# Attention with chunk selection and an ELU MLP: every batch in three query blocks, two head pairs to a PSUM bank

## The chip, the core and the metric

The kernel runs on one core of one Trainium2 chip. The metric is the device time of one execution in microseconds (us). The engines are named as the profile names them: PE (TensorE, matrix multiplies), PEld (its weight loads), DVE (VectorE), ACT (ScalarE), POOL (GpSimd) and SP (SyncE, which here only issues transfers). PSUM is the memory that PE writes and that DVE and ACT read; a bank of it holds 512 float32 numbers on each of 128 partitions.

## The reference

Four batches, eight heads, 768 positions, 64 numbers per head. Keys are cut into chunks of 32; for each query the six chunks with the highest upper bound are kept, and attention runs over those alone, causally. The result, as 3072 rows of 512, goes through an MLP with an ELU between its two products.

```python
chunk, top_k = 32, 6
k_min, k_max = k_chunks.min(axis=3), k_chunks.max(axis=3)
ub = sum(maximum(q * k_min, q * k_max), axis=-1)      # one bound for each query and chunk
top_chunks = argsort(where(causal, ub, -1e9))[..., -top_k:]
scores = where(selected & causal, (q @ k.T) / 8, -1e9)
attn = softmax(scores) @ v
x = attn.transpose(0, 2, 1, 3).reshape(3072, 512)
h = x @ w_in                                          # 512 x 2048
g = where(h > 0, h, exp(minimum(h, 0)) - 1)
out = g @ w_out                                       # 2048 x 512
```

## The kernel before

The work goes block by block. A block is one batch and a range of its queries; `CUTS` (L36) gives batch 0 three blocks of 256 queries and the other batches two of 384, nine blocks in all. The eight heads are handled as four head pairs (`NPAIR`), numbered j: two heads of 64 numbers fill the 128 partitions.

For each block these steps run, each of them a function that records operations:

- **Loads** (`load`, L449 on): 128 queries of all eight heads at a time, 256 KB each, of K, Q and V. For the first three blocks most of them are issued by POOL, and each such issue keeps POOL for about 0.9 us; all later ones are issued by SP. The weights of the MLP are loaded by POOL too, behind the loads of block 1.
- **Preparing K** (`prep_k`, one head pair at a time): PE turns the tiles into one PSUM bank (L501), DVE takes the maximum and the minimum of each chunk of 32 keys (both at L521), and ACT copies the bank out, narrowed to bf16: for blocks 0 and 1 straight into `lhs` (L528, two copies, one for each head), for the others into `kb` (L533), from which SP sends two transfers to `lhs` (L536).
- **Preparing Q** (`prep_q`, one head pair at a time): PE turns the tiles (L501), ACT copies them to `QTf` (L548), two casts bring them to bf16 in `rhs` (for blocks 0 and 1 by ACT, L553, else by POOL, L561), and DVE makes `Qrl`, the positive part (L564).
- **Selecting** (`select`): PE multiplies Q with the chunk bounds (L586, float32), and DVE transposes the result (L597), finds the six best chunks of each query (L604), compares (L608) and transposes the mask into the rows of `rhs` that stand under the queries. Blocks 0 to 2 do that last step with DVE alone (L614); later blocks go through `msk` (L620) and SP transfers (L624).
- **Attending** (`attend`, one head pair at a time): scores (L649; in blocks 0 and 1 the causal triangle is added by a further product, L652), the exponential on ACT (L668, L672), the causal triangle on DVE (L681, L688), the product with V (L703) into one shared bank `o_bank`, the division on DVE (L712, L714) and a transpose into `xt`: for block 0 and the last block by PE (L722) with a copy by DVE (L725), for all others by one transposing transfer on SP's queue (L727).
- **MLP** (`mlp`): 16 slices of 128 of the hidden layer. PE multiplies (L744, four products a slice, as wide as the block has queries); then exp on ACT (L748), an addition on POOL (L750) and the larger or smaller of the two on DVE (L752). Where a block is 256 wide, two slices share a bank and these three run 512 wide. Then each 128 queries are multiplied with `w_out` (L765, sixteen products 512 wide), copied out by ACT (L769) and stored by SP (L772).

The order of all this is not the order of the program text. Each operation is recorded with an engine, an estimated duration, its dependencies and a priority (`plan.op`). `Plan.run` then lets a model of the engines, the transfer queues and the buffers (`CAPS` gives the number of each kind) choose, operation by operation, what each engine does next; the instructions are written in that order, and each engine works through its own list strictly in order. The table `SHIFTS` moves priorities, one number for each kind of operation, engine and block. Operations on one PSUM buffer are put in a chain: a reader waits for the reader before it. Where the model leaves PE idle in the first 70 us, small products on a tile named `junk` are put in (L886).

The front of block i+2 (loads, preparation, selection) is recorded while block i attends, and the MLP of block i stands one block behind.

Of the kernel before, what the change touches and what calls it, by code (L numbers as in the profile page):

```python
# [15 lines left out]
B = 4  # L16
# [19 lines left out]
CUTS = [(0, 256, 512, 768)] + [(0, 384, 768)] * (B - 1)  # L36
BLOCKS = [(b, x, lo, hi) for b in range(B) for x, (lo, hi) in enumerate(zip(CUTS[b], CUTS[b][1:]))]
NBLK = len(BLOCKS)
QMAX = 384
# [25 lines left out]
CAPS = dict(psO=1, psM=7, kld=2, qld=2, vld=1, QTf=6, Qrl=6, kb=3, kmx=2, ubT=2, thr=2,  # L65
            msk=2, pt=9, rcp=2, on=3, xt=12, gT=6, e=4, osb=2)
# [3 lines left out]
EARLY = 30e3  # L70
# [4 lines left out]
    ('cast', 'POOL'): (0.36301, -2.6351, -5.23122, -9.94413, 7.65777, -0.20339, -5.07548, -2.54865, 4.34574),  # L75
    ('gate', 'POOL'): (3.67964, 0.0, 0.0, 0.0, 0.0, 0.0, 0.0, 0.0, 0.0),
    ('init', 'DVE'): (-0.26172, 0.0, 0.0, 6.20378, 8.3173, 3.17992, 8.6172, 2.93233, 6.71757),
    ('init', 'POOL'): (-1.0933, 3.47219, 0.0, 0.0, 0.0, 4.52292, 0.0, 0.0, 0.0),
    ('init', 'SP'): (0.0, 0.0, -0.65038, 0.0, 0.0, 0.0, 0.0, 0.0, 0.0),
    ('kld', 'ACT'): (4.45058, 0.0, 0.0, 0.0, 0.0, 0.0, 0.0, 0.0, 0.0),  # L80
    ('kld', 'SP'): (-2.34682, 0.0, 0.0, 4.79323, 4.52046, -2.14229, -6.13817, -3.59852, -2.65828),
    ('kld', 'POOL'): (0.0, -6.75562, 5.09695, 0.0, 0.0, 0.0, 0.0, 0.0, 0.0),
    ('mlp_in', 'ACT'): (-2.40904, -3.14044, -3.25982, -5.32754, -5.81099, 0.10442, -5.22457, -3.10776, -7.20826),
    ('mlp_in', 'DVE'): (-1.35758, -0.66733, 4.05424, -3.97602, -2.37476, -2.51264, 6.24384, 1.43361, 1.4263),
    ('mlp_in', 'PE'): (2.58869, 0.18485, -0.03717, -4.42605, -1.68403, 0.1887, -0.63691, 0.32029, -2.51407),
    ('mlp_in', 'POOL'): (4.31076, -0.7994, -0.08548, -2.64871, -12.83076, -3.46529, -9.26201, -2.48698, -1.52442),
    ('mlp_out', 'ACT'): (1.82419, -3.05015, -0.78962, -5.55384, -0.16865, -5.05754, 1.41655, -1.16262, -6.87802),
    ('mlp_out', 'PE'): (0.24075, 0.17459, 0.14942, -0.16027, 6.11871, 0.1171, 7.22562, 0.28947, -0.95423),
    ('mlp_out', 'SP'): (-1.76499, -1.716, 5.02829, 3.79669, 6.31947, 8.72257, -1.57087, 0.64556, -8.37831),
    ('prep_k', 'ACT'): (-0.13258, -2.29432, -5.21413, -5.81582, 0.31577, -1.55852, -0.71998, -0.96509, 5.07829),  # L90
    ('prep_k', 'DVE'): (5.88483, 11.93445, -1.39572, -5.21965, -4.45086, -1.35195, -0.53949, -1.64957, -3.66217),
    ('prep_k', 'PE'): (1.96837, 5.99494, 0.08442, 0.09507, 5.41155, -0.21367, -1.89727, 0.49894, 0.29539),
    ('prep_k', 'SP'): (0.0, 0.0, -1.97489, 0.08999, 1.60003, 1.51775, -0.18511, 2.62204, 0.88012),
    ('prep_q', 'ACT'): (-1.1238, -0.17378, -4.62395, -0.38281, -5.63326, -4.36887, 0.60622, 5.30204, 1.20927),
    ('prep_q', 'DVE'): (-1.10909, -11.65783, -10.30533, -1.22248, -15.41771, -10.30347, -8.05233, -0.05077, -3.91546),
    ('prep_q', 'PE'): (-1.9696, -3.23903, -0.01361, -2.1371, -6.53782, -2.99976, -0.67109, 0.13649, 0.01158),
    ('prep_q', 'POOL'): (0.0, 0.0, 11.59933, 3.13777, 1.34215, 2.81799, 3.74405, 9.94498, 5.00197),
    ('qld', 'ACT'): (1.21441, 0.0, 0.0, 0.0, 0.0, 0.0, 0.0, 0.0, 0.0),
    ('qld', 'SP'): (3.66104, 0.0, 0.0, -0.9899, 2.54606, 3.7401, 9.93352, 1.39708, -3.02005),
    ('qld', 'POOL'): (0.0, 3.13091, -1.26946, 0.0, 0.0, 0.0, 0.0, 0.0, 0.0),  # L100
    ('score', 'ACT'): (-7.56297, 0.20574, 8.91891, -5.01381, -2.59914, -0.36508, 1.44839, 2.2134, 3.41788),
    ('score', 'PE'): (0.62726, 0.20683, -0.02773, 0.15303, -0.32678, -2.74631, 0.19235, -0.05167, 0.25745),
    ('score', 'DVE'): (0.0, 0.0, -0.41053, 3.75163, -5.17063, -0.00102, -1.63319, 2.60448, -5.59281),
    ('select', 'DVE'): (-0.39483, -11.74184, -0.31948, -2.00715, -2.53616, -1.49369, 0.2018, 5.38174, -1.32975),
    ('select', 'PE'): (-3.8939, -8.46886, -9.81244, -9.94423, -3.54113, -5.76916, -5.21074, -7.35482, -7.76008),
    ('select', 'SP'): (0.0, 0.0, 0.0, 0.30026, -0.34655, -1.66126, 2.46548, 9.84369, -1.93244),
    ('vld', 'POOL'): (-1.40633, -3.20526, -8.56927, 0.0, 0.0, 0.0, 0.0, 0.0, 0.0),
    ('vld', 'SP'): (0.0, 0.0, 0.0, 0.46689, -0.0871, 2.09994, 4.64846, 3.54379, -2.03203),
    ('w_in', 'POOL'): (-2.40508, 0.0, 0.0, 0.0, 0.0, 0.0, 0.0, 0.0, 0.0),
    ('w_out', 'POOL'): (-6.04092, 0.0, 0.0, 0.0, 0.0, 0.0, 0.0, 0.0, 0.0),  # L110
    ('weigh', 'DVE'): (6.56984, 1.9914, -4.71512, -3.33812, 2.4539, -0.73675, 4.35514, -1.94984, 0.73236),
    ('weigh', 'PE'): (8.24559, -1.30337, -3.1578, -2.868, -0.84271, -0.35438, -0.13752, 4.33018, -0.6965),
    ('weigh', 'SP'): (0.0, -2.66794, -8.47684, -0.40249, -1.54504, -3.77342, -5.02577, -2.38304, 0.0),
# [15 lines left out]
def dve_ns(n):  # L129
    return 68 + 1.03 * n  # L130
# [24 lines left out]
class Plan:  # L155
# [38 lines left out]
    def run(self):  # L194
# [42 lines left out]
        while True:  # L237
# [43 lines left out]
            if done is not None:  # L281
                done.end = clock + (1100 if clock < EARLY else DMA_END)
                lanes[done.eng][done.lane] = done.end
                dirty.update(("SP", "ACT", "POOL"))
                leave(done, done.end)
                enter(done, done.end, True)
                continue
# [28 lines left out]
            else:  # L316
                o.end = t + o.occ + o.lat + (50 if t < EARLY else MARGIN)
# [7 lines left out]
def kernel(  # L325
# [44 lines left out]
    lhs = [fix([P, 2, S], BF16, f"lhs{s}") for s in range(NSET)]  # L370
# [125 lines left out]
    def turn_in(ps, ld, nt):  # L496
        xb, r, hs = ld

        def go():
            for n in range(nt):  # L500
                nc.tensor.transpose(ps.get()[:, P * n:P * (n + 1)],  # L501
                                    xb.get()[:, n, hs, :].rearrange("p h d -> p (h d)"), ident_f)

        op("PE", 15 + 107 * nt, 200, go, reads=[*r, r_ident_f], writes=[ps], hold=[xb])

# [3 lines left out]
    def prep_k(j, i):  # L509
        plan.tag = ("prep_k", i)  # L510
        b, x, lo, hi = BLOCKS[i]
        s, bp, w = (NPAIR * b + j) % NSET, b % 2, hi - lo
        nch = w // CHUNK
        cs = slice(lo // CHUNK, hi // CHUNK)
        k_ld = ldk.pop((j, i))
        psk = buf("psM" if i in PSM_PREP else PS_T, [P, QMAX], F32)
        turn_in(psk, k_ld, w // P)
        kmx = tops[i] = tops[i] if j else buf("kmx", [P, NPAIR, QMAX // CHUNK], F32)

        def reduce(out, o):  # L520
            nc.vector.tensor_reduce(out=out, in_=psk.get()[:, 0:w].rearrange("p (c w) -> p c w", w=CHUNK),  # L521
                                    axis=AX.X, op=o)
# [260 lines left out]
    def front(i):  # L783
        at = span(i - 1, *SP_F)
        for j in range(NPAIR):
            at(j / NPAIR)
            prep_k(j, i)
            prep_q(j, i)
        select(i)
# [128 lines left out]
```

## Time and profile before

Six runs took 289.43, 290.11, 289.97, 290.55, 288.58 and 289.94 us; their median is 289.96 us. The profiled execution is the first of them.

| what | value |
|---|---|
| profiled execution | 289.43 us |
| its span, first to last instruction | 287.6 us |
| around the span | 1.8 us |
| products with `w_out` (L765) | 384, 512 wide |
| products with `w_in` (L744) | 384 of 384 columns, 192 of 256 columns |
| scores (L649) | 120 of 384 columns, 120 of 256, 72 of 128 |
| products with V (L703) | 672 of 65 columns |
| transposes of K and Q (L501) | 192 of 128 columns |
| transposing transfers `xt<-on` (L727) | 28 |
| last product of PE ends | 282.9 us into the span |
| last ACT copy (L769) | 283.0 to 283.6 us |

The page divides the span into forty slices of 7.2 us and gives each engine's busy share of a slice as one digit, tenths rounded down, 9 for 90% and more. "PEclk" gives, in the same way, the clock that PE was granted. A group line gives the line in the kernel, the engine, the operation, what it writes and reads with the shape, how often it ran, its busy time in us and the mean of one in ns. The mean of a PE product holds the way through the array, in which the next product already runs, so the pace of a run of products is taken from the timeline instead: from the start of the first to the start of the last.

### The profile page before, as it was taken

To read this page: it belongs to the slowest core of one execution; us is meant where nothing else is said; L and a number is where in the kernel's file an instruction comes from. 1 tells how busy PE (TensorE), PEld (TensorE's weight loads), DVE (VectorE), ACT (ScalarE), POOL (GpSimd) and SP (SyncE) were. 2 spreads that over 40 slices of the span, in tenths; PEclk is the share of its full clock that TensorE was granted. 3 is DMA by queue.
4 is the path that set the end of the run, shared out by engine and by line. 5 is a ranking of instruction groups with operands and counts; after the bars stand their busy time and mean duration, and the time that the engine had idled before them with its cause. 6 is when DMAs were issued, how large, how long until landed. Compare 5 with 4: busy or idle time off the path is not lost.

```text
span 287.6 us, 7048 instructions
## 1 busy us (share of the span) xinstructions
PE 271.4 (94%) x2491; PEld 176.8 (61%) x2519; DVE 191.2 (66%) x608; ACT 194.7 (68%) x434; POOL 130.2 (45%) x256
## 2 busy tenths in 40 slices
PE   6787989999999999999999999999999999999993
PEld 5565765697686666766556656656765566555541
DVE  8865998848579957578588965633698647425420
ACT  2995583998287798876865568767974498665530
POOL 8679870068086007654067525531681224204600
PEclk9577999999999999999999999999999999999999
DMA  8899999559847245994289627951212310020031
GB/s 193 229 231 196 289 208 125 128 158 207 183 111 170 51 68 119 227 229 95 53 206 226 133 49 167 210 154 56 68 25 77 82 50 3 0 73 2 0 112 74
DMA packets 86883, 36.22 MB, mean 126 GB/s; under 512 B 74176, under 2 KB 82880, under 8 KB 86848
## 3 DMA queue, kind: packets, MB, share of 16 engines
q1 hardware_dynamic: 79424, 27.38, 40.8%
q0 software_dynamic: 5344, 7.87, 13.4%
q10 hardware_dynamic: 2080, 0.52, 0.8%
q8 instruction: 20, 0.33, 0.5%
q14 instruction: 15, 0.12, 0.1%
HBM read 27.26 MB, written 6.29 MB: 117 GB/s over the span
## 4 chain that ended last, share of the span: by engine, by line
PE 72%; DMA 8%; DVE 7%; POOL 5%; ACT 3%; issue 2%; SPq 1%; POOLq 0%; ACTq 0%
PE psM L765 25%; PE psM L744 22%; PE psM L649 10%; PE o_bank L703 6%; PE psM L501 6%; DMA vld<-in_v_dram 5%; PE psM L586 2%; DVE gT L752 2%; ACT pt L668 2%; DMA xt<-on 2%; POOL kld L463 1%; POOL vld L463 1%; DVE rhs L614 1%; DMA kld<-in_k_dram 1%; POOL vext L492 1%
## 5 line engine op out<-in xcount | busy, mean ns | idle before, releaser
L750 POOL TENSOR_SCALAR e<-e 128x384 f32<-128x384 f32 (+1 forms) x120 | 63.6, 537 | 87.4 <-ACT e L748 62.0
L765 PE MATMUL psM<-w_out_sb,gT 128*128 128x512 bf16 x356 | 93.4, 379 | 1.0
L744 PE MATMUL psM<-xt,w_in_sb 128*128 128x384 bf16 (+1 forms) x576 | 92.9, 311 | 0.8 <-DMA xt<-on 0.6
L668 ACT ACTIVATE pt<-psM 128x384 bf16<-128x384 f32 (+1 forms) x168 | 80.9, 563 | 17.2 <-PE psM L649 16.4
L752 DVE SCALAR_TENSOR_TENSOR gT<-psM,e 128x384 bf16<-128x384 f32 (+1 forms) x120 | 67.3, 579 | 33.1 <-POOL e L750 26.3
L748 ACT ACTIVATE e<-psM 128x384 f32<-128x384 f32 (+1 forms) x120 | 62.2, 530 | 29.8 <-PE psM L744 28.9
L744 PEld LDWEIGHTS <-w_in_sb 128*128 128x128 bf16 x576 | 56.1, 99 | 29.5 <-issue 2.7
L649 PE MATMUL psM<-rhs,lhs 96*128 96x256 bf16 (+2 forms) x312 | 58.4, 281 | 1.2 <-DVE rhs L614 0.5
L765 PEld LDWEIGHTS <-gT 128*128 128x128 bf16 x384 | 36.0, 97 | 30.6 <-DVE gT L752 0.6
L561 POOL TENSOR_SCALAR rhs<-QTf 64x384 bf16<-64x384 f32 (+1 forms) x56 | 28.6, 510 | 42.9 <-ACT QTf L548 39.4
L649 PEld LDWEIGHTS <-lhs 96*128 96x128 bf16 x312 | 28.6, 98 | 16.8 <-DVE rhs L614 0.8
L703 PEld LDWEIGHTS <-pt 128*128 128x128 bf16 x672 | 26.6, 97 | 8.1 <-issue 1.3
L769 ACT ACTIVATE osb<-psM 128x512 f32<-128x512 f32 x24 | 14.4, 606 | 23.2 <-PE psM L765 13.7
L703 PE MATMUL o_bank<-vext,pt 128*128 128x65 bf16 x672 | 29.2, 193 | 0.1
L521 DVE TENSOR_REDUCE kmx<-psM 128x12 f32<-128x384 f32 (+1 forms) x36 | 17.6, 503 | 7.5 <-PE psM L501 7.4
L548 ACT ACTIVATE QTf<-psM 128x384 f32<-128x384 f32 (+1 forms) x36 | 15.4, 471 | 10.6 <-PE psM L501 10.4
L492 POOL TENSOR_SCALAR vext<-vld 128x384 bf16<-128x384 f32 (+1 forms) x36 | 16.6, 482 | 9.6 <-DMA vld<-in_v_dram 8.9
L681 DVE TENSOR_TENSOR pt<-pt,tri 128x512 bf16<-128x512 bf16 x28 | 12.2, 436 | 11.9 <-ACT pt L668 11.7
L533 ACT ACTIVATE kb<-psM 128x384 bf16<-128x384 f32 (+1 forms) x28 | 14.2, 509 | 6.7 <-DVE kst L521 4.1
L714 DVE TENSOR_TENSOR on<-o_bank,rcp 128x384 bf16<-128x384 f32 (+1 forms) x36 | 18.3, 507 | 0.8
L501 PE MATMUL psM<-ident_f,qld 128*128 128x128 f32 x96 | 16.1, 300 | 2.4 <-DMA qld<-in_q_dram 0.8
L521 DVE TENSOR_REDUCE kst<-psM 128x12 f32<-128x384 f32 (+1 forms) x36 | 17.5, 500 | 0.6 <-PE psM L586 0.5
(56 smaller groups left out, 204.8 us busy)
## 6 DMA issues: line engine op xcount, KB each, us to landing
out_dram<-osb SPq DMA_DIRECT2D x24, 256.0 KB, 2.3
kld<-in_k_dram SPq DMA_DIRECT2D x19, 256.0 KB, 4.1
qld<-in_q_dram SPq DMA_DIRECT2D x19, 256.0 KB, 3.6
vld<-in_v_dram SPq DMA_DIRECT2D x18, 256.0 KB, 4.2
lhs<-kb SPq DMA_DIRECT2D x48, 48.0 KB, 2.0
w_in_sb<-in_moe_w_in_dram POOLq DMA_DIRECT2D x4, 512.0 KB, 10.5
w_out_sb<-in_moe_w_out_dram POOLq DMA_DIRECT2D x4, 512.0 KB, 10.8
vld<-in_v_dram POOLq DMA_DIRECT2D x6, 256.0 KB, 5.5
```

Source lines behind the costliest of these rows:

```text
L492: return op("POOL", pool_ns(hi - lo), 60, lambda: nc.gpsimd.tensor_scalar(out=vexts[s][:, lo // P:hi // P, :, 0:D], in0=xb.get()[:, 0:nt, ...
L501: nc.tensor.transpose(ps.get()[:, P * n:P * (n + 1)], xb.get()[:, n, hs, :].rearrange("p h d -> p (h d)"), ident_f)
L521: nc.vector.tensor_reduce(out=out, in_=psk.get()[:, 0:w].rearrange("p (c w) -> p c w", w=CHUNK), axis=AX.X, op=o)
L561: pool_op(110 + pool_ns(w), lambda h=h: nc.gpsimd.tensor_scalar(out=rhs[RH[i]][0:64, h, j, 0:w], in0=qtf.get()[64 * h:64 * h + 64, 0:w], s ...
L649: nc.tensor.matmul(sps.get()[:, o + pc:o + pc + n], lhsT=lhs[s][0:96, hd, P * kb:P * (kb + 1)], rhs=rhs[y][0:96, hd, j, c0 - lo:c0 - lo + ...
L668: op("ACT", act_ns(wtot), 140, lambda pt=pt, sps=sps, hd=hd, wtot=wtot: nc.scalar.activation(out=pt.get()[:, hd, 0:wtot], in_=sps.get()[:, ...
L703: nc.tensor.matmul(o3.get()[:, hd, qi, :], lhsT=pt.get()[:, hd, P * qt + off:P * qt + off + P], rhs=vexts[s][:, kb, hd, :], start=(kb == 0 ...
L744: op("PE", 1 + w / 2.4, 200, lambda fc=fc, kk=kk, h_ps=h_ps, o=w * (fc - f0): nc.tensor.matmul(h_ps.get()[:, o:o + w], lhsT=w_in_sb[:, kk, ...
L748: op("ACT", act_ns(m * w), 200, lambda e=e, h_ps=h_ps: nc.scalar.activation(out=e.get()[:, 0:m * w], in_=h_ps.get()[:, 0:m * w], func=AF.E ...
L750: op("POOL", pool_ns(m * w), 72, lambda e=e: nc.gpsimd.tensor_scalar(out=e.get()[:, 0:m * w], in0=e.get()[:, 0:m * w], scalar1=-1.0, scala ...
L752: g = op("DVE", dve_ns(m * w), 130, lambda e=e, h_ps=h_ps, f0=f0: nc.vector.scalar_tensor_tensor(out=gT[f0 // 4].get()[:, f0 % 4:f0 % 4 + ...
L765: op("PE", 216, 200, lambda tt=tt, fc=fc, o_ps=o_ps: nc.tensor.matmul(o_ps.get(), lhsT=gT[fc // 4].get()[:, fc % 4, P * tt:P * (tt + 1)], ...
```

## The change

All batches are cut into three blocks of 256 queries, so there are twelve blocks and none of 384. Two head pairs, j and j+1, then share one PSUM bank in `prep_k` and `prep_q`: four transposes fill it, and one maximum, one minimum, one copy and one pair of casts work on 512 columns where two of each worked on 256. For that, the eight `lhs` tiles become slices of one tile `lhs_all`, so that one copy or one transfer can write two head pairs. `QTf` and `Qrl` hold two head pairs each, and `qf` says at which column a pair begins. In the MLP nothing is edited, but with 256 queries every pair of hidden slices shares a bank, so L748, L750 and L752 are always 512 wide. `CAPS` loses one `kb` buffer and gains one `pt`. The model's constants for the first microseconds change (`EARLY`, the landing time of an early transfer, the early margin), and `SHIFTS` holds new numbers for twelve blocks.

```diff
-CUTS = [(0, 256, 512, 768)] + [(0, 384, 768)] * (B - 1)
+CUTS = [(0, 256, 512, 768)] * B
-QMAX = 384
+QMAX = 256
-CAPS = dict(psO=1, psM=7, kld=2, qld=2, vld=1, QTf=6, Qrl=6, kb=3, kmx=2, ubT=2, thr=2,
-            msk=2, pt=9, rcp=2, on=3, xt=12, gT=6, e=4, osb=2)
+CAPS = dict(psO=1, psM=7, kld=2, qld=2, vld=1, QTf=6, Qrl=6, kb=2, kmx=2, ubT=2, thr=2,
+            msk=2, pt=10, rcp=2, on=3, xt=12, gT=6, e=4, osb=2)
-EARLY = 30e3
+EARLY = 16e3
 SHIFTS = {
-    ('cast', 'POOL'): (0.36301, -2.6351, -5.23122, -9.94413, 7.65777, -0.20339, -5.07548, -2.54865, 4.34574),
+    ('cast', 'POOL'): (-0.01023, -0.19778, -2.85537, -2.16881, 5.58036, 0.56984, 1.90469, -0.13243, 0.34306, 0.29503, -0.39182, 5.85763),
...
-                done.end = clock + (1100 if clock < EARLY else DMA_END)
+                done.end = clock + (800 if clock < EARLY else DMA_END)
...
-                o.end = t + o.occ + o.lat + (50 if t < EARLY else MARGIN)
+                o.end = t + o.occ + o.lat + (40 if t < EARLY else MARGIN)
...
-    lhs = [fix([P, 2, S], BF16, f"lhs{s}") for s in range(NSET)]
+    lhs_all = fix([P, NSET, 2, S], BF16, "lhs")
+    lhs = [lhs_all[:, s, :, :] for s in range(NSET)]
...
+    def turn_in(ps, lds, nt):
+        for z, (xb, r, hs) in enumerate(lds):
+            def go(z=z, xb=xb, hs=hs):
+                for n in range(nt):
+                    nc.tensor.transpose(ps.get()[:, P * (nt * z + n):P * (nt * z + n + 1)],
+                                        xb.get()[:, n, hs, :].rearrange("p h d -> p (h d)"), ident_f)
+            op("PE", 15 + 107 * nt, 200, go, reads=[*r, r_ident_f], writes=[ps], hold=[xb])
...
     def prep_k(j, i):
+        m = 512 // w
+        js = range(j, j + m)
+        psk = buf("psM", [P, 512], F32)
+        turn_in(psk, [ldk.pop((z, i)) for z in js], w // P)
-        op("DVE", dve_ns(w), 115, lambda: reduce(kmx.get()[:, j, 0:nch], AOT.max), reads=[psk], writes=[kmx])
+        op("DVE", dve_ns(m * w), 115, lambda: reduce(kmx.get()[:, j:j + m, 0:nch], AOT.max), reads=[psk], writes=[kmx])
...
+                op("ACT", 60 + act_ns(m * w), 90, lambda h=h: nc.scalar.activation(
+                    out=lhs_all[0:64, sets[0]:sets[0] + m, h, lo:hi],
+                    in_=psk.get()[64 * h:64 * h + 64, 0:m * w].rearrange("p (m w) -> p m w", m=m), func=AF.Copy),
+                    reads=[psk], writes=[r_lhs[s][x] for s in sets])
...
     def front(i):
         at = span(i - 1, *SP_F)
-        for j in range(NPAIR):
+        for j in range(0, NPAIR, 512 // (BLOCKS[i][3] - BLOCKS[i][2])):
             at(j / NPAIR)
             prep_k(j, i)
             prep_q(j, i)
```

What is left out of the diff follows the same pattern: the minimum, the `kb` copy with its two transfers (each now writes two head pairs, in runs of 512 bytes where they were 768), the `QTf` copy, the casts, `Qrl`, and in `select` the column at which a head pair begins. In the changed kernel the lines shift by about eleven: L744 becomes L755, L765 becomes L776, L649 becomes L660, L614 becomes L625, L727 becomes L738.

## The prediction, made before the changed kernel ran

> **What bounds the kernel now.** I read the page's busy shares and slices first, then a table of stretches that I cut where the character of the run changes, then who waited for whom on PE alone, and last the timeline of PE for its pace.
>
> ```profile
> span 287.6 us, 7048 instructions
> PE 271.4 (94%) x2491; PEld 176.8 (61%) x2519; DVE 191.2 (66%) x608; ACT 194.7 (68%) x434; POOL 130.2 (45%) x256
> ...
> PE   6787989999999999999999999999999999999993
> ...
> PEclk9577999999999999999999999999999999999999
> ```
>
> PE is the only engine near full, and it misses time only in the first six slices and in the last one. The stretches say how much (columns: length; busy time and number of instructions of PE, PEld, DVE, ACT, POOL; granted clock; transfer share; GB/s):
>
> ```profile
> 8.00:17.00 9.00, 7.35 (x60) 4.76 (x59) 7.08 (x33) 8.76 (x27) 5.95 (x10) 0.50 0.91 234
> 17.00:25.00 8.00, 5.02 (x70) 4.25 (x68) 4.34 (x17) 7.01 (x20) 6.30 (x11) 0.93 1.14 206
> 25.00:29.00 4.00, 4.00 (x52) 2.76 (x49) 1.53 (x5) 1.19 (x2) 3.69 (x5) 0.66 1.24 206
> 29.00:33.00 4.00, 4.00 (x51) 3.29 (x35) 3.88 (x23) 1.89 (x4) 2.98 (x6) 1.00 1.12 305
> 33.00:37.00 4.00, 3.04 (x27) 2.07 (x24) 3.77 (x11) 3.32 (x7) 3.94 (x6) 1.00 1.12 259
> 37.00:41.00 4.00, 3.28 (x38) 2.48 (x38) 3.97 (x9) 2.79 (x9) 2.88 (x9) 1.00 1.24 206
> 41.00:45.00 4.00, 3.95 (x59) 3.21 (x57) 3.30 (x14) 4.00 (x11) 1.98 (x5) 1.00 1.24 209
> 45.00:283.00 238.00, 235.30 (x2123) 149.31 (x2148) 156.73 (x485) 163.21 (x354) 95.76 (x185) 1.00 0.47 109
> ```
>
> From 45 us on PE has 235.3 of 238 us at full clock. From 8 to 17 us ACT is the full engine (8.76 of 9.00). From 29 to 41 us it is DVE (3.88, 3.77 and 3.97 of 4.00), while PE lacks 0.96 and 0.72 us; just before, from 25 to 29, DVE lies idle for 2.5 us. What PE itself waited for from 45 us to the end of its work is the whole answer of the next view, and it is 1.0 us:
>
> ```profile
> PE psM L744 <- DMA xt<-on: 0.6, 1, 0.6
> PE psM L649 <- DVE gT L752: 0.2, 1, 0.2
> PE psM L649 <- issue: 0.2, 1, 0.2
> ```
>
> So a cheaper ACT, DVE or POOL is worth nothing after 45 us. The change can win before 45 us, and must pay for whatever it adds to PE anywhere. The pace of PE:
>
> ```profile
> 60.45 4.53 PE L744 MATMUL psM<-xt,w_in_sb 128*128 128x256 bf16 x40
> 106.83 5.36 PE L744 MATMUL psM<-xt,w_in_sb 128*128 128x384 bf16 x32
> ```
>
> Less the last product's own 0.28 and 0.33 us, and over 39 and 31 steps, a 256-wide product takes 109.0 ns and a 384-wide one 162.3 ns.
>
> **The change, PE first.** In the MLP 384 products of 384 columns become 576 of 256: 576 x 109.0 - 384 x 162.3 = 62.78 - 62.32 = +0.46 us. The scores keep their columns (2,688 a head and batch) but come in 384 instead of 312 products; the same step of about 2.4 ns for a further product (3 x 109.0 - 2 x 162.3) gives 72 x 2.4 = +0.17 us. The chunk bounds (L586) go from two blocks to three in batches 1 to 3. In the chain of waits a whole set took 0.81 us at 192 queries and 1.45 at 384, so 3.33 ns a query and 0.17 us fixed: 0.38 at 64 queries and 1.02 at 256. Three batches of (0.38 + 2 x 1.02 - 0.81 - 1.45) = +0.5 us. The last block has two tiles to turn instead of three for each head pair: four transposes less, at 56 ns in the timeline, -0.2 us. Products with V, with `w_out`, and the transposes of K and Q keep number and size. PE's floor rises by 0.9 us, all on the path. Here nothing hides it: PE is full.
>
> **The first 45 us.** Batch 0 has the same three blocks and the same loads as before, so what changes there is how many instructions ACT and DVE run. For widths that the trace lacks I take the slope between the 384- and 512-wide rows of L748 (509 and 614 ns, 0.82 ns a column): 16 copies at L528 (5.4 us together) become 8 of 0.34 + 0.21 = 0.55 us, 16 at L553 (5.6 us) become 8 of 0.56, and 8 at L548 (0.375 each) become 4 of 0.585. ACT saves 1.0 + 1.1 + 0.7 = 2.8 us in blocks 0 and 1. Little of it is on the path: the first exponential at 17.56 us stands behind the `QTf` copy at 17.02, and that behind the transposes of block 1's Q, which run from 14.72 to 16.98 at half clock and come after the chunk bounds of block 0 in the old order and in the new. What remains is the run of eight exponentials: in the old order a cast (0.41 us) sits between the seventh and the eighth, in the new one none does, and the first division at 20.20 us waits for the product with V behind them. I take 0.5 us, bounds 0 (the eighth score is late anyway) and 1.0 (the copies too end sooner).
>
> DVE's 24 reductions of batch 0 become 12: 24 x 0.396 = 9.5 us before, and by the slope of the 256- and 384-wide rows (416 and 545 ns) 12 x 0.67 = 8.0 after, -1.5 us, -0.4 of it between 29 and 45. More is moved than saved. In the new instruction order, PE runs the chunk bounds of block 1 ahead of all 48 first MLP products; before, they stood behind 17 of them, at half clock, and began at 28.28 us. The result then reaches DVE at about 26 us, and the transposes (0.77 us) and best-of-eights (1.22 us) fall into DVE's idle 2.5 us instead of into the full stretch from 29 us. They must also wait for `Qrl` of block 1, which DVE now makes ahead of the last `xt` copy; that copy moves back by up to 1.0 us, of which 0.56 was a wait, and PE has the bounds to run in that gap. So the full DVE stretch ends about 2.0 + 0.4 us sooner. PE can take of that what it lacked from 33 to 45 us, 0.96 + 0.72 + 0.05 = 1.7 us. Bounds: 0, if the ELU at L763, which now stands among the mask transposes in DVE's list, holds them up while waiting for POOL (L750 kept DVE waiting 2.4 us there before), and 2.4, if DVE's whole gain counts. I take 1.7, since DVE has no other releaser in that stretch than itself. Together the first 45 us give 2.2 us, bounds 0 and 3.4.
>
> One skill rule speaks against sharing a bank. The trace has ACT waiting for DVE at L533 behind a minimum for 4.1 us in three places, and no PE wait behind it after 45 us. The Trainium skill, "PSUM — Partial Sum Buffer", section "PSUM bank collisions raise a hardware error", says that two engines must never be on one bank and the same quarter of its partitions at once, reads against reads included. So ACT may not copy the first head pair while DVE reduces the second: by the rule the first pair's copy is later by two transposes and two half reductions, about 0.22 + 0.54 us as an estimate from this trace's rows, and were that exposed in each of blocks 0 to 2 the gain would shrink by 2.3 us to nothing. The trace's rows speak for zero, since ACT has a `QTf` copy to run meanwhile.
>
> **What is hidden.** After 45 us, by the group rows: DVE's ELU 67.3 to 96 x 0.6625 = 63.6 us, reductions -1.5, triangles 19.2 to 17.4, but divisions and their reciprocals (48 each instead of 36) +3.9; together -3. ACT: exp of the MLP 62.2 to 58.0, `kb` about -2, `QTf` -0.7. POOL: ELU 63.6 to 60.0, casts -2, V casts +1.4. All of it lies under PE, which waits 1.0 us in 238; if that cover went, they would count. SP's queue gets heavier: 12 more transposing issues of 1.2 us, 24 more masks of about 0.55, 16 fewer `lhs` transfers: 14.4 + 13 - 9 = +18 us. Loads keep their number, and SP's largest wait is for ACT's output copies, so the queue has room; bounds 0 and the rival below. The end keeps its shape: last copy 0.6 us, last store, 4.6 us from the last product to the span's end.
>
> Sum against the profiled execution: 289.43 + 0.9 - 2.2 = 288.1, which is 1.8 under the median of 289.96.
>
> **Rivals.** (1) *The loads hide the gain.* From 17 to 45 us the transfer share is 1.12 to 1.24 on the slices' scale, the highest of the run, and K of block 1 is what PE waited for at 10.70. For it: the bytes of batch 0 are unchanged. Against it: from 33 to 41 us PE's waits name ACT and DVE, no load. Time: 289.43 + 0.9 - 0.3 = 290.0, no difference.
>
> (2) *The narrower blocks run out of cover for `xt`* (slower). A block's MLP starts only when the last head pair has gone through reciprocal (0.18), division (0.42) and the transposing transfer (2.7 us to landing, longest 6.3). Counting PE's work, at the paces above, between a block's last product with V and its first MLP product in the instruction orders of the two built kernels, the old one has 4.4 to 6.6 us for blocks 2 to 7 and yet one wait of 0.6; the new one has 4.2 to 5.0 for blocks 1, 2, 4 and 10. For it: SP is in order, and each transfer may stand behind masks and loads. Against it: four old blocks with 4.4 to 5.0 us had no wait. Price: four waits of 1.2 us, 288.1 + 4.8 = 292.9; it decides from a sum of 2.7 us on, two such waits and a bit.
>
> (3) *The start gains more*: softmax chain 1.0, DVE 2.4, and one of the half-clock windows (0.50 from 8 to 17 us, 0.66 from 25 to 29) shrinks by 1 us of PE time. 289.43 + 0.9 - 4.4 = 285.9. For it: the granted clock follows how busy PE is in this trace; against it: PE's order there is nearly the old one.
>
> **How the numbers follow.** A measurement of this kernel tells 0.3%, 0.9 us, from no change. Forecast 0.42, rival 1 0.23, rival 2 0.19, rival 3 0.16. The likeliest is 288.1. Its own range, by the bounds of the start, is 286.9 to 290.3; the range for 8 in 10 reaches to 285.9 for rival 3 and to 291.0 into rival 2, which leaves out about half of it and a little of rival 3. Faster: most of the forecast and rival 3, 0.57; same: rival 1 and the forecast's upper part, 0.24; slower: rival 2, 0.19.
>
> **What would show it.** Right: the MLP's products with `w_in` at 109 ns start to start; PE full from about 43 us and DVE idle for under 1 us between 25 and 29; waits of PE after 45 us at 2 us or less; the last product about 1.3 us sooner than 282.9. Wrong: `PE psM L755 <- DMA xt<-on` with several us (rival 2); PE waits for loads or a half-clock stretch beyond 29 us (rival 1); or an end that moves although the first 45 us did not, which no step here covers.

## The result, and the profile after

The changed kernel takes 292.02 us (median of 35 runs; 289.91 to 295.0) against 290.53 us for the kernel before (72 runs): the ratio is 1.005, 95% interval 1.0032 to 1.0068. It is slower by half a per cent, 1.5 us, and lies above the range of the prediction, 285.9 to 291.0 us. Ratios, here and below, compare only executions within 1.5% of the fastest of the same kernel, while medians take all of them. The profiled execution took 292.12 us (span 290.3), the one of before 289.43 (span 287.6).

The page of the changed kernel, busy shares and slices:

```profile
span 290.3 us, 7697 instructions
PE 270.0 (93%) x2846; PEld 200.5 (69%) x2878; DVE 188.3 (65%) x581; ACT 188.1 (65%) x374; POOL 125.9 (43%) x228
...
PE   6578798999999999998999999999899999999994
...
PEclk9887999999999999999999999999999999999999
```

Past 50 us there are now two slices where PE's digit is 8 (from 130.6 and from 203.2 us); before there was none. The table of stretches of the changed kernel (columns as in the prediction):

```profile
25.00:29.00 4.00, 3.97 (x42) 2.56 (x27) 2.11 (x19) 1.19 (x2) 1.40 (x2) 0.84 1.22 197
29.00:33.00 4.00, 2.55 (x24) 2.05 (x23) 2.69 (x5) 1.79 (x3) 3.03 (x6) 1.00 1.18 261
33.00:45.00 12.00, 11.37 (x124) 9.34 (x122) 11.59 (x25) 10.92 (x23) 9.13 (x17) 1.00 1.18 243
45.00:283.00 238.00, 232.47 (x2459) 171.61 (x2489) 153.67 (x474) 157.77 (x315) 91.79 (x160) 1.00 0.45 108
```

From 33 to 45 us PE does more, as forecast, though not as much: 11.37 us against 10.27 before, +1.1 where 1.7 was put. But it loses 1.45 us from 29 to 33, and from 45 to 283 us it is busy 232.47 us where it was 235.30: 2.8 us are lost in the stretch in which nothing was expected to change. (Both traces lack records of some products with `w_out`, 28 before and 32 after, so the waits are the surer measure.) Who PE waited for there, in the changed kernel:

```profile
PE psM L501 <- DMA kld<-in_k_dram: 1.7, 4, 0.9
PE psM L660 <- DMA rhs<-msk: 0.9, 1, 0.9
PE psM L660 <- DVE rhs L625: 0.7, 1, 0.7
PE psM L501 <- DMA qld<-in_q_dram: 0.2, 1, 0.2
PE psM L776 <- issue: 0.2, 1, 0.2
```

K and Q that have not landed, five times, and one mask. No wait for `xt` is among them. Before, the whole list came to 1.0 us, now it is 3.7. The timeline of PE in the changed kernel shows the largest wait for K (137.12), the gap at the start (31.32), and the pace of bounds and MLP:

```profile
25.74 4.13 PE L755 MATMUL psM<-xt,w_in_sb 128*128 128x256 bf16 x32
31.32 1.37 PE L755 MATMUL psM<-xt,w_in_sb 128*128 128x256 bf16 x11 [1.45 <-DMA w_in_sb<-in_moe_w_in_dram]
...
77.45 0.66 PE L597 MATMUL psM<-QTf,kst 64*32 64x256 f32 x16
77.90 0.64 PE L597 MATMUL psM<-Qrl,kst 64*32 64x256 f32 x16
78.47 0.36 PE L714 MATMUL o_bank<-vext,pt 128*128 128x65 bf16 x6
...
135.95 0.30 PE L501 MATMUL psM<-ident_f,kld 128*128 128x128 f32 x1
137.12 0.99 PE L501 MATMUL psM<-ident_f,kld 128*128 128x128 f32 x7 [0.87 <-DMA kld<-in_k_dram]
...
265.59 7.15 PE L755 MATMUL psM<-xt,w_in_sb 128*128 128x256 bf16 x64
```

And SP's timeline ahead of that wait:

```profile
127.41 3.07 SPq L635 DMA_DIRECT2D rhs<-msk  x5
130.58 0.53 SPq L783 DMA_DIRECT2D out_dram<-osb  x1
131.16 0.67 SPq L539 DMA_DIRECT2D lhs<-kb  x1
131.93 1.19 SPq L464 DMA_DIRECT2D kld<-in_k_dram  x2
133.22 2.75 SPq L464 DMA_DIRECT2D qld<-in_q_dram  x2
136.06 1.56 SPq L738 DMA_TRANSPOSE xt<-on  x1
```

SP issues without a pause: five masks, a store, an `lhs` transfer, then four loads of 256 KB. The second K load goes out at 132.5 us; PE turns the first tile at 135.95, wants the second 0.30 us later and gets it at 137.12. Meanwhile the transfer engines are full. Busy tenths of the 16 engines from 131 to 138 us, in forty slices of 0.175 us, changed kernel:

```profile
DMA  0204999428502447999999999999996234689999
```

From 133.8 to 136.2 us every slice is a 9. I call *cover* the time from the issue of a block's last K (or Q) load to PE's first turn of it. From the issues and starts in the traces: before, K had 11.8, 6.0, 4.9, 5.1 and 25.6 us (blocks 4 to 8) and Q 4.3 to 5.3 (blocks 4 to 7); now K has 4.9, 3.5, 5.2, 3.4, 7.8, 6.0, 4.1 and 4.0 us (blocks 4 to 11), and Q 3.0 to 5.1. The median landing of SP's loads is 3.9 us for K and 4.3 for Q (before, 4.1 and 3.6). The cover has shrunk to the landing time.

### The profile page after: what moved, and what is told of

Read it like the earlier page. It is cut to its first block, busy times and chain, and to the rows that moved or that the text cites. A ratio compares the mean times of both kernels' runs of the same rounds, so it can differ in the third digit from the quotient of the medians.

```text
span 290.3 us, 7697 instructions
## 1 busy us (share of the span) xinstructions
PE 270.0 (93%) x2846; PEld 200.5 (69%) x2878; DVE 188.3 (65%) x581; ACT 188.1 (65%) x374; POOL 125.9 (43%) x228
## 3 DMA queue, kind: packets, MB, share of 16 engines
q0 software_dynamic: 5344, 7.87, 12.9%
## 4 chain that ended last, share of the span: by engine, by line
PE 60%; DMA 17%; DVE 6%; POOL 5%; SPq 4%; ACT 4%; issue 3%; ACTq 0%; POOLq 0%
PE psM L755 21%; PE psM L776 20%; PE psM L660 8%; DMA kld<-in_k_dram 8%; DMA w_in_sb<-in_moe_w_in_dram 5%; PE psM L501 5%; PE o_bank L714 5%; ACT pt L679 2%; PE psM L597 2%; DMA rhs<-msk 2%; DMA vld<-in_v_dram 2%; SPq L464 1%; DVE gT L763 1%; SPq L635 1%; DMA qld<-in_q_dram 1%
## 5 line engine op out<-in xcount | busy, mean ns | idle before, releaser
L679 ACT ACTIVATE pt<-psM 128x512 bf16<-128x512 f32 (+1 forms) x192 | 91.1, 606 | 16.6 <-PE psM L660 13.8
L776 PE MATMUL psM<-w_out_sb,gT 128*128 128x512 bf16 x352 | 95.5, 379 | 1.2 <-issue 0.2
L761 POOL TENSOR_SCALAR e<-e 128x512 f32<-128x512 f32 x96 | 59.4, 622 | 83.1 <-ACT e L759 66.7
L755 PE MATMUL psM<-xt,w_in_sb 128*128 128x256 bf16 x768 | 92.0, 273 | 1.5 <-DMA w_in_sb<-in_moe_w_in_dram 1.4
L759 ACT ACTIVATE e<-psM 128x512 f32<-128x512 f32 x96 | 57.9, 604 | 44.2 <-PE psM L755 40.7
L763 DVE SCALAR_TENSOR_TENSOR gT<-psM,e 128x512 bf16<-128x512 f32 x96 | 63.8, 682 | 34.1 <-POOL e L761 23.6
L755 PEld LDWEIGHTS <-w_in_sb 128*128 128x128 bf16 x768 | 73.8, 98 | 14.4 <-DMA w_in_sb<-in_moe_w_in_dram 2.0
L660 PE MATMUL psM<-rhs,lhs 96*128 96x256 bf16 (+1 forms) x384 | 58.2, 259 | 2.7 <-DMA rhs<-msk 0.9
L776 PEld LDWEIGHTS <-gT 128*128 128x128 bf16 x384 | 35.5, 98 | 26.3 <-issue 0.4
L660 PEld LDWEIGHTS <-lhs 96*128 96x128 bf16 x384 | 34.7, 98 | 18.6 <-issue 1.9
L572 POOL TENSOR_SCALAR rhs<-QTf 64x512 bf16<-64x512 f32 x40 | 26.0, 650 | 40.1 <-ACT QTf L555 36.7
L493 POOL TENSOR_SCALAR vext<-vld 128x256 bf16<-128x256 f32 x48 | 19.2, 423 | 19.0 <-DMA vld<-in_v_dram 18.7
L725 DVE TENSOR_TENSOR on<-o_bank,rcp 128x256 bf16<-128x256 f32 x48 | 20.0, 417 | 0.9
## 6 DMA issues: line engine op xcount, KB each, us to landing
w_in_sb<-in_moe_w_in_dram POOLq DMA_DIRECT2D x4, 512.0 KB, 12.9
```

The costliest lines, as they stand in the source:

```text
L572: pool_op(110 + pool_ns(m * w), lambda dst=dst, src=src: nc.gpsimd.tensor_scalar(out=dst(), in0=src(qtf), scalar1=1.0, scalar2=0.0, op0=AO ...
L660: nc.tensor.matmul(sps.get()[:, o + pc:o + pc + n], lhsT=lhs[s][0:96, hd, P * kb:P * (kb + 1)], rhs=rhs[y][0:96, hd, j, c0 - lo:c0 - lo + ...
L679: op("ACT", act_ns(wtot), 140, lambda pt=pt, sps=sps, hd=hd, wtot=wtot: nc.scalar.activation(out=pt.get()[:, hd, 0:wtot], in_=sps.get()[:, ...
L725: op("DVE", dve_ns(w), 140, lambda: nc.vector.tensor_tensor(out=on.get()[:, 0:nt, :, :].rearrange("p q h d -> p h q d"), in0=o3.get()[:, : ...
L755: op("PE", 1 + w / 2.4, 200, lambda fc=fc, kk=kk, h_ps=h_ps, o=w * (fc - f0): nc.tensor.matmul(h_ps.get()[:, o:o + w], lhsT=w_in_sb[:, kk, ...
L759: op("ACT", act_ns(m * w), 200, lambda e=e, h_ps=h_ps: nc.scalar.activation(out=e.get()[:, 0:m * w], in_=h_ps.get()[:, 0:m * w], func=AF.E ...
```

## The experiments

Ratios are to the kernel before, run on the same chip; the changed kernel's own is 1.005. A difference of 0.001 is 0.29 us.

**Is it the loads?** In the changed kernel, with its order kept, the second K and Q tile of blocks 3 to 11 is not loaded (half_loads), or loaded with one head of eight (small_loads):

```diff
+                if i >= 3 and n == 1 and cls != "vld":
+                    return
...
-                                        xb.get()[:, n, hs, :].rearrange("p h d -> p (h d)"), ident_f)
+                                        xb.get()[:, 0 if xb.one else n, hs, :].rearrange("p h d -> p (h d)"), ident_f)
```

> The changed kernel with every instruction in its place, but for blocks 3 to 11 the second 128-query tile of K and of Q is not loaded and the first is turned twice (so the output of those blocks is not the reference's). That takes 18 issues of about 0.6 us, 11 us, off SP's list, and half the bytes of those loads. Theory A (SP's list is so full that K, Q and mask transfers reach PE late): in the changed kernel's profile PE loses about 3 us more than the old one after 45 us, most of it at L501 and one wait for a mask; here the L501 waits for K and Q after 45 us fall from 1.9 us on PE to under 0.5, and the time falls by 2 to 3 us, to about 289.5. Theory B (the 1.5 us are the 0.9 us of further PE work and a start that lost its gain to late w_in slices): the time stays within 0.7 us of the changed kernel's 292.0.

> As half_loads (288.35, ratio to before 0.9945), but the second K and Q tile of blocks 3 to 11 is still issued, with one head of eight: the 18 issues are back on SP's list, the bytes stay away. (Output of those blocks not the reference's.) If it is SP's issue time that makes the transfers late, the time goes back to the changed kernel's, ratio 1.002 to 1.006. If it is the bytes on the transfer engines, it stays with half_loads, ratio 0.993 to 0.997. In between says both.

half_loads: 288.35 us, ratio 0.9945 [0.9922, 0.9969]. small_loads: 288.17 us, 0.9913 [0.9874, 0.9951]. The issues are back in the second and the gain stays, so it does not come from fewer issues; fewer bytes are enough. But not only the bytes changed: the small loads also hold SP for less (the K and Q issues after 45 us take 19.9 us in small_loads, 28.1 in the changed kernel and 10.1 in half_loads). PE's waits from 45 us on in half_loads:

```profile
PE psM L663 <- DVE rhs L628: 0.7, 1, 0.7
PE psM L504 <- DVE gT L766: 0.6, 1, 0.6
PE psM L663 <- DMA rhs<-msk: 0.4, 2, 0.2
PE psM L779 <- issue: 0.2, 1, 0.2
```

No load is left in the list. The wait for `w_in` at 31 us is gone too (landing 10.3 us instead of 12.9), but not to PE's profit: half_loads starts the chunk bounds of block 2 at 45.30 us, the changed kernel at 45.06, so the gain lies behind 45 us. But fewer bytes might help any version, so the kernel before got a like cut (before_fewer, the second tile of three in blocks 3 to 8: 12 issues and a third of the bytes, where the new kernel lost 18 issues and half):

> Control: the old kernel with every instruction in its place, but the second K and Q tile of blocks 3 to 8 not loaded (12 issues and a third of those bytes away; output of those blocks not the reference's). If late loads are a loss of the new kernel alone, as theory A has it, the old one gains at most what it waited at L501 after 45 us, 0.3 us: ratio 0.998 to 1.000. If fewer loads help any kernel of this kind, it gains 1 us or more as the new one did (ratio 0.996 or less), and half_loads says little on the change.

289.12 us, 0.9966 [0.9932, 1.0001]. The cut is worth about 0.003 to the old kernel and 0.011 to 0.014 to the new one (1.005 less 0.9945 and 0.9913). The difference, 0.007 to 0.010 or 2 to 3 us, is more than the whole loss of 1.5 us. Enlarged in the ratio of the issues, 18 to 12, the old kernel's gain would be 0.005 and the difference 1.6 to 2.5 us, still no less than the loss; with intervals of 0.002 to 0.004 on each ratio no more can be told.

**Is it the early loads of block 3, which pass while `w_in` lands?** They go out between 15 and 22 us. late_q3 moves SP's loads of block 3's Q to just before the first `kb` transfer, near 40 us; late_q3_half does that and half_loads.

```diff
+    tail = [o for o in plan.order if o.key[0] == ("qld", 3)]
+    first = next(o for o in plan.order if o.key == (("prep_k", 2), "SP"))
+    plan.order = [o for o in plan.order if o not in tail]
+    at = plan.order.index(first)
+    plan.order[at:at] = tail
```

> The changed kernel with every instruction in its place but two: SP's loads of block 3's Q, issued at 15.6 us into the w_in loads, stand directly before SP's first kb transfer (at about 40 us). Theory B: those 512 KB took bandwidth from w_in; without them PE's wait of 1.4 us for the third w_in slice goes below 0.3 us, and the time falls by 1.0 to 1.5 us, to about 290.7. Theory A: PE may lose the wait, but DVE is full from 29 to 41 us and what PE gains it gives back to DVE there; the time falls by less than 0.5 us.

> Both edits together (output of blocks 3 to 11 not the reference's). If the two losses are separate, the gains add: 3 to 4 us below the changed kernel, 288 to 289. If a stall removed early only moves on to the next late transfer, the time is no better than the better of the two alone.

291.53 us, 1.0049 [1.0016, 1.0082], and 288.78 us, 0.9962 [0.9941, 0.9983]. PE still waits 1.5 us for `w_in` in late_q3. Moving Q alone changes nothing, and adds nothing to half_loads. Block 3's K was not moved.

**Is it the number of buffers of K and Q?** three_bufs makes a load tile as large as it is used and has three of each; the planner makes a new order.

```diff
-        xb = buf(cls, [P, 3, H, D], F32)
+        xb = buf(cls, [P, 2, H, D], F32)
-CAPS = dict(psO=1, psM=7, kld=2, qld=2, vld=1, QTf=6, Qrl=6, kb=2, kmx=2, ubT=2, thr=2,
+CAPS = dict(psO=1, psM=7, kld=3, qld=3, vld=1, QTf=6, Qrl=6, kb=2, kmx=2, ubT=2, thr=2,
```

> The changed kernel, correct, with load tiles of two 128-query tiles (a block needs no more) and, in about the same memory, three K and three Q load buffers instead of two; the planner makes a new order from that. Theory A in the form that loads are late because a buffer comes free late: PE waits less at L501 after 45 us (under 0.7 us) and the time falls by 1 to 3 us. Theory A in the form that SP's list itself is late: little or no change, since the list is as long. The new order adds an unknown of its own of perhaps 1 to 2 us either way.

292.73 us, 1.0104 [1.0069, 1.0139]. The planner did not use the third buffer to load earlier: K's cover is still 3.4 to 4.9 us in blocks 4 to 7, so this run does not test whether buffers hold the loads back. That two buffers allow far earlier loads is seen in early_kq, below.

**What if SP's queue is lighter?** ACT instead of SP issues the 24 output stores, in place, in the changed kernel (after_act_stores) and in the one before (before_act_stores):

```diff
-nc.sync.dma_start(out=out[r0:r0 + P, :], in_=osb.get())
+nc.scalar.dma_start(out=out[r0:r0 + P, :], in_=osb.get())
```

> The changed kernel, correct, with every instruction in its place, but the 24 stores of the output are issued by ACT, which makes what they store, in place of SP. SP's list loses 24 issues of 0.53 us, 13 us, and the 40 us in which it stood before a store waiting for ACT's copy, with everything behind that. Theory A: the waits for K, Q and masks after 45 us fall below 1.5 us in all and the time by 1.5 to 2.5 us, ratio to before 0.996 to 1.000. Theory B: no change (ratio 1.005); ACT pays 12 us of issue time, which may cost up to 1 us where ACT is on the path.

> The same edit on the old kernel, correct. Theory A: it had 1.0 us of waits after 45 us, so at most that is gained, ratio 0.997 to 1.000; if ACT's 12 us of issues are on the path, ratio 1.000 to 1.004. A gain as large as the new kernel's would mean that SP's list bound the old kernel just as much.

289.19 us, 0.9968 [0.9935, 1.0001], and 289.83 us, 0.9993 [0.995, 1.0036]. The new kernel gets 0.008 (2.4 us) from it, the old one nothing that can be told. PE's waits from 45 us on in after_act_stores:

```profile
PE psM L660 <- DVE rhs L625: 0.7, 1, 0.7
PE psM L501 <- DMA qld<-in_q_dram: 0.5, 1, 0.5
PE psM L660 <- DMA rhs<-msk: 0.3, 1, 0.3
PE psM L755 <- DMA xt<-on: 0.2, 1, 0.2
```

1.7 us where the changed kernel has 3.7. That is a little over theory A's 1.5; the time is as theory A said. K's cover is 6.0, 4.4, 6.0, 4.3, 9.1, 6.5, 4.7 and 4.8 us, longer in every block, by 0.5 to 1.3 us. So with all bytes loaded, about a microsecond more cover a block goes with 2.0 us less waiting; a store issue ahead of the loads holds SP for 0.53 us.

**Do the loads only stand at the wrong place?** All SP loads are in one chain, and V has one buffer, so K and Q of the next block stand behind V's hand-over. early_kq takes the K and Q loads of blocks 4 to 11 to a place ahead of that V load. early_kq_act adds the stores on ACT.

```diff
+    for i in range(4, NBLK):
+        mine = [o for o in plan.order if o.key[0] in (("kld", i), ("qld", i))]
+        old = [o for o in plan.order if o.key in ((("prep_k", i - 2), "PE"), (("prep_q", i - 2), "PE"))]
+        first = next(o for o in plan.order if o.key[0] == ("vld", i - 1))
...
+                plan.order[at:at] = mine
```

> The changed kernel with the K and Q loads of blocks 4 to 11 moved ahead of the V loads of the block before them in SP's list (about one hand-over, some 10 us, earlier); nothing else moves and all bytes are loaded. Theory (the loads are late only because they stand behind V's one buffer in SP's list): PE's waits for kld and qld at L501 after 45 us fall from 1.9 us to under 0.3, and the time to 288.5 to 290, ratio to the kernel before 0.995 to 1.000. Rival A (the queue as a whole is too full, so an earlier K or Q only delays masks, lhs or stores): the waits move to L660 and L755 and the ratio stays at 1.003 or above. Rival B (the two K and Q buffers are what holds the loads back, not their place in the list): the loads wait for PE's turns at the new place, the masks behind them come late, ratio 1.005 or above.

> The edit of early_kq together with the 24 output stores issued by ACT instead of SP. Theory: both remove the same waits, so the gains overlap: ratio 0.993 to 0.997, little below the one with the stores alone (0.9968). Rival (the two are separate costs): the gains add to about 0.992.

305.28 us, 1.0483 [1.0432, 1.0535], and 298.73 us, 1.0283 [1.0229, 1.0336]. My theory fell, and by a lot. K and Q now have 14 to 33 us of cover in blocks 4 to 10, and PE does not wait for them. It waits for the rest, for masks and `xt` as rival A said, and for `gT`, which no theory named, in early_kq:

```profile
PE psM L660 <- DMA rhs<-msk: 4.6, 4, 3.5
PE psM L501 <- DVE gT L763: 3.0, 2, 2.4
PE psM L755 <- DMA xt<-on: 2.6, 3, 1.6
```

Its SP timeline shows why:

```profile
81.98 1.39 SPq L464 DMA_DIRECT2D kld<-in_k_dram  x2
83.48 2.05 SPq L464 DMA_DIRECT2D qld<-in_q_dram  x2
85.63 1.94 SPq L464 DMA_DIRECT2D vld<-in_v_dram  x1
87.66 1.52 SPq L738 DMA_TRANSPOSE xt<-on  x1
89.27 5.02 SPq L635 DMA_DIRECT2D rhs<-msk  x8
```

Five loads in a row hold SP for 5.6 us. The eight masks behind them go out from 89.27 us; in the changed kernel they went out from 82.80. PE's timeline of early_kq:

```profile
87.24 0.35 PE L714 MATMUL o_bank<-vext,pt 128*128 128x65 bf16 x6
91.12 0.98 PE L660 MATMUL psM<-rhs,lhs 96*128 96x256 bf16 x6 [3.53 <-DMA rhs<-msk]
```

After the 3.53 us the granted clock (third number from the end) halves, from 92.5 to 99.3 us, and again after a wait of 2.41 us that ends at 238.87:

```profile
92.50:99.30 6.80, 6.25 (x31) 3.63 (x30) 3.07 (x7) 4.99 (x11) 0.53 (x2) 0.50 0.26 59
99.40:102.00 2.60, 2.60 (x17) 1.37 (x16) 0.05 (x1) 1.73 (x4) 1.05 (x3) 1.00 0.00 0
...
239.30:242.70 3.40, 3.29 (x12) 1.28 (x11) 3.00 (x6) 1.56 (x3) 1.63 (x3) 0.50 0.55 122
```

So such a wait is paid twice. Of the 13.2 us between the two profiled runs, the listed waits explain 10.9 - 3.7 = 7.2 (with 0.7 for L625), and the 10.2 us at half clock, in which PE was busy for 9.5, some 4.8, an estimate.

**Queue or transfer engines?** act_loads has ACT issue the K and Q loads of blocks 4 to 11, at their old places; act_loads_stores the stores too; early_act has early_kq's places.

```diff
+                if i >= 4 and cls != "vld":
+                    q = nc.scalar
```

> The changed kernel with the K and Q loads of blocks 4 to 11 (32 of 256 KB) issued by ACT instead of SP; they keep their places in the written order, and all bytes are loaded. Theory (SP's single queue is what makes them late): loads no longer wait behind SP's masks, transposing transfers and V loads, L501's load waits after 45 us fall from 1.9 us to under 0.3 and no other transfer gets late, ratio to the kernel before 0.992 to 0.998. Rival A (the transfer engines are what is short at that moment): the loads land as late as before, ratio 1.002 to 1.007. Rival B (ACT reaches the places in its own list later than SP did, or the loads now wait on ACT for PE's turns and hold up the exponentials behind them): waits for pt or kld grow, ratio above 1.005.

> act_loads and the 24 output stores issued by ACT too. Theory: either move alone removes the same lateness, so both together give little more than the better one, ratio 0.991 to 0.997. Rival: ACT's list, now with 56 issues more, holds up exponentials and copies, ratio above that of the stores alone (0.9968).

> The early places of early_kq (K and Q loads of blocks 4 to 11 ahead of the V loads of the block before), but issued by ACT, so that SP's list holds none of them. Theory Q (SP issues one thing after another, so an early load made the masks behind it late): without SP's issues masks and transposing transfers come in time, PE's waits after 45 us fall under 2 us, ratio 0.993 to 0.999. Theory E (the loads' bytes occupy the transfer engines that all queues share, so masks that are sent at the same moment land late whoever issued the loads): L660 waits for msk of 2 us or more, half-clock stretches, ratio above 1.01 as with early_kq (1.048).

296.18 us, 1.0114 [1.0064, 1.0164], a wide spread (292.14 to 299.26; the medians alone give 1.021); 290.77 us, 0.9989 [0.9949, 1.0028]; and 305.87 us, 1.0461 [1.0397, 1.0526]. In act_loads K's cover is longer than in the changed kernel in every block (4.7 to 5.6 us in blocks 4 to 7), and no wait for K is left. Q's is not (3.3 to 5.4 in blocks 4 to 11, and 0.5 to 0.8 shorter in blocks 4, 6, 7 and 8):

```profile
PE psM L503 <- DMA qld<-in_q_dram: 1.6, 2, 1.0
PE psM L757 <- DMA xt<-on: 1.1, 1, 1.1
PE psM L503 <- ACT QTf L557: 0.7, 1, 0.7
```

Taking 32 issues off SP did not bring Q in time, so the theory fell as it was written. Q did not land later than in the changed kernel (after 45 us a median of 3.9 us against 4.2) but was issued nearer to its use, which is closer to rival B than to rival A; this profile is of an execution of 293.74 us and doesn't show what the slower ones lost. The Trainium skill, "DMA: Bandwidth & Descriptors", section "Issuing engines are not separate DMA queues", says that transfers of all engines run on the same 16 DMA engines and that another issuer saves only the issue time. No run here shows that sharing by itself. But early_act shows that the issue itself is not cheap. ACT's timeline:

```profile
52.69 1.01 ACTq L466 DMA_DIRECT2D kld<-in_k_dram  x2
53.90 3.00 ACTq L466 DMA_DIRECT2D qld<-in_q_dram  x2
56.94 1.09 ACT L681 ACTIVATE pt<-psM 128x512 bf16<-128x512 f32 x2 [3.66 <-issue]
```

Four loads in a row keep their issuer for 4.2 us, whichever it is; here the exponentials stood behind them, PE waited 3.0 us for `pt`, and from 57.6 to 61.0 us the granted clock was 0.50. Theory Q fell. Each sign of theory E came (2.9 us of waits for masks in three places, half clock, 1.046), but the largest waits are for `pt`, 3.0 and 1.9 us, of which it does not speak, so it is at most a part of the cause.

**Would a small move do?** near_sp moves the loads ahead by 4 us of the planner's time, near_act the same with ACT as issuer, near_sp_stores near_sp with the stores on ACT.

```diff
+            at = next(x for x, o in enumerate(plan.order) if o.start >= mine[0].start - 4000)
```

> The K and Q loads of blocks 4 to 11 still issued by SP, moved ahead by 4 us of the planner's time, past some masks and transposing transfers. Theory Q (one queue for all): what is won at L501 is lost at L660 or L755, ratio 1.000 to 1.010. Rival (the place alone was wrong): L501 waits under 0.3 us and nothing else late, ratio 0.993 to 0.998.

> The K and Q loads of blocks 4 to 11 issued by ACT and moved ahead in the written order by 4 us of the planner's time. Theory (the loads land just too late at their old places, and a little cover is all that lacks): cover grows to 7 to 9 us, PE's waits for kld and qld after 45 us go, ratio 0.993 to 0.999. Rival (loads of ACT hold ACT's list up, or masks come late): ratio above 1.003.

> near_sp with the 24 output stores issued by ACT. Theory: the stores leave room on SP's queue for the earlier loads, ratio 0.992 to 0.997, not above the stores alone (0.9968). Rival: the masks passed by the loads are late even so, ratio above 1.000.

313.82 us, 1.0773 [1.0715, 1.083]; 314.27 us, 1.0727 [1.0653, 1.0801]; 310.54 us, 1.0672 [1.0622, 1.0723]. All worse than the large move. In near_sp PE waits 7.2 us for masks in four places (longest 3.4), 2.9 for `gT` and 2.7 for `xt`, and four half-clock stretches of 3.4 us follow. The edit moves K and Q each on its own, which put Q ahead of K in several blocks, so the size is not that of a clean 4 us; all six kernels that load earlier are slower.

**Which half of the change is it?** blocks_alone has twelve blocks, but one head pair to a bank (`m = 1`, with twice as many `QTf`, `Qrl` and `kb` of half the size).

> Three blocks of 256 in every batch, but one head pair per PSUM bank as before: the copies, casts and reductions are 256 wide again, twice as many (QTf and Qrl have 12 buffers of half the size, kb four); the planner makes its own order from the same priorities. Theory (what costs is the twelve blocks' transfers on SP's queue, and sharing a bank is beside the point after 45 us): as slow as the changed kernel or slower, ratio 1.003 to 1.015, PE waits for kld, qld or msk after 45 us again 2 us or more. Rival (sharing a bank costs, since ACT and DVE take the shared bank in turn): the ratio is 1.000 or below.

313.06 us, 1.0768 [1.0723, 1.0814]. This doesn't separate the two halves: the planner's new order makes PE wait 7.8 us for a K load between 30 and 45 us, with the clock at 0.50 from 31 to 41 us, a loss that neither theory speaks of. After 45 us it lists 5.5 us of waits, 2.6 of them for K and masks. The opposite half, sharing without new cuts, wasn't tried.

## Why the prediction was wrong, point by point

**The step that failed** is under "What is hidden": "Loads keep their number, and SP's largest wait is for ACT's output copies, so the queue has room; bounds 0". The sum of the added issues was nearly right: SP's issues from 45 us on last 171.3 us in all against 148.6 before, +22.7 where I had +18. Two things were wrong. First, room on average is not room where it counts: the wait for output copies lies in eight places, while ahead of the K load at 131.93 SP did not pause once. Second, I counted issues and never asked by how much the *loads* of K and Q lead their use. Before, some covers were already 4.3 to 5 us at landings near 4; one column of the same table would have shown that a microsecond more ahead of the loads turns into waits.

**PE's floor, +0.9 us**: it holds. 64 MLP products take (7.15 - 0.28) / 63 = 109.0 ns each, and a set of bounds for 256 queries lasts from 77.45 to 78.47, the 1.02 us of the sum. Counted over the weight loads of the two traces, at these paces, PE's work grows by 0.9 us, fillers apart.

**The first 45 us, -2.2 us**: the mechanism came as described, the gain was over-sized. The bounds of block 1 run at 23.86 instead of 28.28 us, and the last turn for `xt` comes 1.2 us sooner (23.50 against 24.70; I had 0.5). But the first slices of the MLP then ran out of weights: the third slice of `w_in` lands at 31.3 us instead of 29.4, and PE waits 1.45 us. DVE is idle 1.9 us from 25 to 29, not under 1. At 45 us both kernels have the same work left by that count, so in these two profiles the start gained just the added 0.9 us, where I had 2.2. Rival 3's larger gain did not come. The wait for `w_in`, a sign of rival 1, is not what was missing: early_kq, with the same instructions up to there, has no such wait and yet starts the bounds of block 2 later (before, changed kernel, early_kq):

```profile
45.25 0.66 PE L586 MATMUL psM<-QTf,kst 64*32 64x256 f32 x16
45.06 0.66 PE L597 MATMUL psM<-QTf,kst 64*32 64x256 f32 x16
45.38 0.66 PE L597 MATMUL psM<-QTf,kst 64*32 64x256 f32 x16
```

One profile of each is thin evidence here. In before_act_stores, whose start is that of the old kernel, the same products begin at 46.62 us. So the start of the profile before was a good one, and the usual gain may be larger than 0.9; that would fit 2.7 us more of waits after 45 us beside a loss of 1.5 between the medians, but no run shows it.

**What is hidden, but for SP**: from 45 to 283 us DVE has 3.1 and POOL 4.0 us less, as forecast, ACT 5.4 less where I had about 7, and all of it lies under PE.

**The rule on PSUM banks**: in the first 45 us of the changed kernel the only wait of ACT for DVE on the list is 0.5 us at L530, and not for a reduction; a price of 2.3 us does not show. No run here isolates the rule itself.

**Rival 2** has the right sign and the right resource, SP's list with narrower blocks, but the wrong transfer: after 45 us `xt` is not on PE's list of waits, K, Q and one mask are. That its time, 292.9, is nearly the measured one is luck. The line that I had named as the sign of it would not have shown; "an end that moves although the first 45 us did not, which no step here covers" is what happened. The changed kernel's last product ends at 286.55 us instead of the forecast 281.6, 3.65 later than before. The waits after 45 us are 2.7 of that; 0.95 I can't assign. The end behind it did not keep its shape: from the start of the last copy to the end of the span there are 3.7 us where there were 4.6, which hides those 0.95 in the spans.

**What stays open**: what sharing a bank is worth by itself; how much of the lateness is SP's time and how much the time on the transfer engines, since fewer bytes and fewer other issues both remove it; why act_loads is slower than the changed kernel while the stores on ACT help; and whether an order planned anew with the stores on ACT would beat the old kernel by more than after_act_stores, whose interval still touches 1.

## What to carry to other kernels

When a change cuts work into smaller blocks, list for every transfer how long before its use it is issued, beside how long it takes to land; here the smallest of these differences decided, not the room on the queue as a whole. In this list, in which masks and `xt` come just in time too, no load could be moved forward for nothing: six attempts ended 8 to 23 us above the kernel before, by what they passed on SP's list, or by what they held up on ACT's. Taking something unneeded out of the way, here stores on which PE never waited, recovered the loss.

## What the runs showed of the hardware

In early_kq a PE wait of 2.41 us was enough for the clock to halve for the next 3.4 us (239.3 to 242.7), and after one of 3.53 us it was halved for 6.8 us; the changed kernel's waits after 45 us, 0.9 us at most, left it alone. Length alone does not settle it. Over all runs, each of the nine waits of 2.9 us and more after 45 us came with a half-clock stretch, but of the 14 between 1.4 and 2.5 us only five did: 1.60 us in blocks_alone and 1.73 in early_act, for instance, but not 2.32 in near_sp or 2.45 in near_sp_stores. The Trainium skill, "TensorE: Matmul & The Clock Gate", section "What's actually happening", has the clock drop after an idle window of about 3.4 us; here shorter gaps could do it.

Back to back, loads of 256 KB in 256-byte runs hold their issuer: in early_act 0.38 us for the first, 0.59 for the second, and 3.00 us for the third and fourth together.
